# Strassen products summed in PSUM with partial sums copied out between, GpSimd taken out of the token pairs, row block by row block

## The chip, the cores and the metric

One Trainium2 chip, of which the kernel uses one core. The time is the device time of one execution in microseconds (us). Before the change it is 1486.4 us, the median of 3 runs (1483.56 to 1487.43).

## The reference

```python
def reference(**kw):                       # B, H, S, D = 8, 8, 576, 64; d_model 512
    attn_out = _attn_ref(q, k, v)          # block-causal softmax attention
    x = attn_out.transpose(0, 2, 1, 3).reshape(B, S, H * D)
    x = _moe_ref(x, w_val, conv_w, w_out)  # sigmoid(conv(x)) * (x @ w_val) @ w_out
    return _moe2_ref(x, w_ch1, w_ch2)

def _moe2_ref(x, w_ch1, w_ch2):
    X = np.fft.fft(np.fft.fft(x, axis=1), axis=2)
    u = x + np.real(X)
    un = (u - mean(u)) / np.sqrt(var(u) + 1e-06)
    ch = np.maximum(un @ w_ch1, 0.0) @ w_ch2      # 512 -> 2048 -> 512
    return u + ch
```

What matters here is the last line but one: two matrix products with a normalisation before them, for 8 x 576 = 4608 tokens. Every product of numbers of 32 bits is made of three matmuls of a rounded form: high part of the weights with the high and with the low part of the tokens, and the low part of the weights with the high part of the tokens.

## The kernel before, in words

`phase1` does attention, the gated convolution and the Fourier transforms and leaves u in DRAM (`u_d`). `phase2` does the normalisation and the two layers. Its first 1024 tokens are done in two groups of 512 with plain products (loop `for g in range(NG)`). While the second group runs, `combine` forms the sums and differences of weight blocks that Strassen's method wants and stores them in DRAM (`comb_d`, beside the plain blocks in `base_d`).

The other 3584 tokens are done in NQ = 4 *pairs*. A pair is two blocks of N = 448 tokens, and for a pair each layer is one Strassen step (Winograd's form, 2 x 2 blocks): the weights are cut in halves by rows and by columns, the tokens into the two blocks, and seven products stand in place of eight. A pair's work is the list `steps`: (g, l, p, i) is pair g, layer l, product p, row block i, and one step is 12 matmuls of 448 columns (lines 1333 to 1335 in the first layer, 1359 to 1361 in the second). Seven products of four row blocks are 28 steps a layer, 56 a pair, 224 in all: 2688 matmuls. The order of products is `L1O`, `L2O`; within a product the four row blocks i follow each other.

Around the steps:

- `load_chunk` loads the weights of two steps (1 MB) from DRAM into one of six places (`ring_w`); a chunk is asked for five chunks ahead.
- `load_x` loads the next pair's tokens X into one of two sets of places, which take turns, and `norm_x` normalises them, a piece after each step, part of it on GpSimd (POOL). `average` (lines 1107, 1108) puts two matmuls with a matrix of ones on TensorE for each mean.
- `sums` makes a product's operand: Strassen's sums of X blocks in the first layer, of h blocks in the second, all on POOL (lines 1277 to 1287). `operand` splits it into high part (ScalarE cast, line 1303) and low part (VectorE, line 1304), three steps ahead (`LOOK`).
- `product` issues the 12 matmuls and takes the result out of PSUM. In the first layer each product lies in one of three bank pairs in turn, and VectorE adds it to running sums h in SBUF (lines 1344, 1346; Relu on ScalarE, line 1349). In the second layer four steps sum up in a bank pair, and VectorE and POOL add the result to e and to the output rows y (lines 1370 to 1389), which `load_y` has filled with u and `store_y` sends out.

The program's text gives a rough order only: a scheduler in the framework puts the instructions of each engine's queue in order. Within a queue order is strict, and so a waiting instruction holds up all behind it; SyncE (SP) issues all the transfers.

Of the kernel before, what the change touches and what calls it, by code (L numbers as in the profile page):

```python
# [8 lines left out]
F32 = mybir.dt.float32  # L9
# [8 lines left out]
def kernel(  # L18
# [1030 lines left out]
    def phase2():  # L1049
        with ExitStack() as c2:  # L1050
# [60 lines left out]
            def norm(u, n, done, hl=None, first=False, pool=None):  # L1111
                pool = pool or nc.vector
# [116 lines left out]
            L1O, L2O = (1, 6, 2, 7, 5, 3, 4), (1, 3, 5, 2, 6, 7, 4)  # L1229
            steps = [(g, l, p, i) for g in range(NQ) for l in range(2) for p in (L1O, L2O)[l] for i in range(4)]  # L1230
# [3 lines left out]
            ring_w = [4, 5, 6, 7, 8, 9]  # L1234
            ring_o = [10, 11, 12, 13]
# [3 lines left out]
            def load_chunk(c):  # L1239
                if 2 * c >= len(steps):  # L1240
                    return
                g, l, p, i = steps[2 * c]
                z = i // 2
                chunk[c] = at(ring_w[c % 6], [P, 4, 2, 256], F32R, "chunk")
                src = SRC[l, p][z][SLOT[l, p]] if (l, p) in SRC else comb_d[l][z][SLOT[p]]
                nc.sync.dma_start(out=chunk[c].bitcast(F32).rearrange("p j y c -> p (j y c)"), in_=src)

            def load_x(g):
                if g >= NQ:
                    return  # L1250
                for z in range(2):
                    n = (2, 3) if g % 2 == 0 else ("U1", "HH")
                    X[g, z] = at(n[z], [P, 4, N], F32, f"X{z}")
                    load_rows(X[g, z], NG * T + 2 * N * g + N * z, N, 0, 4)

            def norm_x(g):
                if g >= NQ:
                    return
                for z in range(2):
                    def scale(r, u=X[g, z]):  # L1260
                        for t in range(4):
                            (nc.gpsimd if t % 2 else nc.vector).tensor_tensor(  # L1262
                                out=u[:, t, :], in0=u[:, t, :], in1=r, op=ALU.mult)
                            yield
                    yield from norm(X[g, z], N, scale, None, False, nc.gpsimd)
# [3 lines left out]
            def sums(k):  # L1269

                g, l, p, i = steps[k]
                if l == 0:
                    xa, xb = X[g, 0], X[g, 1]
                    b11, b21, b12, b22 = xa[:, 0:2], xa[:, 2:4], xb[:, 0:2], xb[:, 2:4]
                    if p == 6:
                        T2[g] = t2 = s3.tile([P, 2, N], F32, tag="st", name="T2")
                        nc.gpsimd.tensor_tensor(out=b12, in0=b12, in1=b11, op=ALU.subtract)
                        nc.gpsimd.tensor_tensor(out=t2, in0=b22, in1=b12, op=ALU.subtract)
                    elif p == 7:
                        nc.gpsimd.tensor_tensor(out=b11, in0=T2[g], in1=b11, op=ALU.subtract)  # L1280
                    elif p == 4:
                        nc.gpsimd.tensor_tensor(out=b21, in0=T2[g], in1=b21, op=ALU.subtract)
                    return {1: b11, 6: T2.get(g), 2: b21, 7: b11, 5: b12, 3: b22, 4: b21}[p]
                a, b, c, d = (hb[z][i // 2][:, i % 2 * 2:i % 2 * 2 + 2] for z in range(4))
                x, y, z = {5: (b, b, a), 6: (d, d, b), 7: (a, d, a), 4: (c, d, c)}.get(p, (None,) * 3)
                if x is not None:
                    nc.gpsimd.tensor_tensor(out=x, in0=y, in1=z, op=ALU.subtract)  # L1287
                return {1: a, 3: d, 5: b, 2: c, 6: d, 7: a, 4: c}[p]

            src, nitem = {}, [0]  # L1290

            def operand(k):
# [4 lines left out]
                if l == 0 and i:  # L1297
                    opnd[k] = opnd[k - 1]
                    return
                x = src.pop(k) if k in src else sums(k)  # L1300
                o = at(ring_o[nitem[0] % 4], [P, 2, 2, N], F32R, "o")
# [7 lines left out]
            def load_y(g, q):  # L1309
                col = NG * T + 2 * N * g + N * (q in (12, 22))  # L1310
                for m in range(2):
                    if q == 21 and m == 0:
                        Y["pair"] = yp.tile([P, 2, N], F32, tag="y", name="y")
                    Y[q, m] = y = (Y["pair"][:, m] if q == 21 else
                                   kp.tile([P, S], F32, tag={12: "K0", 22: "K1", 11: "KP"}[q], name="y")[:, 0:N])
# [6 lines left out]

            def product(k):
                g, l, p, i = steps[k]
                o, w = opnd.pop(k), chunk[k // 2]
                if l == 0:
                    ps = banks[(k + 2) % 3]
                    for jj in range(2):
                        j = i % 2 * 2 + jj
                        for t in range(2):  # L1330
                            wh, wl = (w[:, j, y, t * P:t * P + P] for y in range(2))
                            to = ps[:, jj, 0:N]
                            nc.tensor.matmul(to, wh, o[:, 0, t], start=(t == 0), stop=False)  # L1333
                            nc.tensor.matmul(to, wh, o[:, 1, t], start=False, stop=False)  # L1334
                            nc.tensor.matmul(to, wl, o[:, 0, t], start=False, stop=(t == 1))  # L1335
                    ps = ps[:, :, 0:N]
                    a, b, c, d = (hb[z][i // 2][:, i % 2 * 2:i % 2 * 2 + 2] for z in range(4))
                    if p == 1:
                        nc.scalar.copy(out=a, in_=ps)  # L1339
                        return  # L1340
                    for to, x in {6: ((b, a),), 2: ((a, a),), 7: ((c, b),), 5: ((d, c), (b, b)), 3: ((b, b),),
                                  4: ((c, c),)}[p]:
                        if p == 4:
                            nc.vector.tensor_tensor(out=to, in0=x, in1=ps, op=ALU.subtract)  # L1344
                        else:
                            nc.vector.tensor_tensor(out=to, in0=ps, in1=x, op=ALU.add)  # L1346
                    if p in (2, 5, 3, 4):
                        h = {2: a, 5: d, 3: b, 4: c}[p]
                        nc.scalar.activation(out=h, in_=h, func=AF.Relu)  # L1349
                    return  # L1350

                ps = banks[(k // 4 + 2) % 3]
                for jj in range(2):
                    j = i % 2 * 2 + jj
                    for m in range(2):
                        wh, wl = (w[:, j, y, m * P:m * P + P] for y in range(2))
                        to = ps[:, m, 0:N]
                        first, final = i == 0 and jj == 0, i == 3 and jj == 1
                        nc.tensor.matmul(to, wh, o[:, 0, jj], start=first, stop=False)  # L1359
                        nc.tensor.matmul(to, wh, o[:, 1, jj], start=False, stop=False)  # L1360
                        nc.tensor.matmul(to, wl, o[:, 0, jj], start=False, stop=final)  # L1361
                if i < 3:
                    return
                add, sub = ALU.add, ALU.subtract
# [224 lines left out]
```

## Time and profile before

| | |
|---|---|
| median of 3 runs | 1486.4 us |
| the profiled execution: its time, its span | 1490.79 us, 1489.0 us |
| granted TensorE clock, mean | 0.977 |
| busy share PE, DVE, ACT, POOL | 93%, 80%, 53%, 36% |
| matmuls of the four pairs | from 883.2 us to 1484.8 us |
| after the last matmul | two VectorE adds, two stores |

A busy time counts every instruction from its start to its modelled end. Matmuls overlap, so that their pitch (start to start, about 0.205 us here) and not their duration (0.37 us) tells how long TensorE needs. An idle time is put down to the instruction that ended it.

### The profile page before, as it was taken

What the parts mean: (1) busy time and instruction counts of PE and PEld (TensorE: products, weight loads), DVE (VectorE), ACT (ScalarE), POOL (GpSimd) and SP (SyncE); (2) the same over time, 40 slices, a digit from 0 to 9 for tenths busy, and PEclk for the clock granted to TensorE, in tenths of its full rate; (3) what the DMA queues carried; (4) which work ended last, traced back from release to release, by engine and by line L of the source; (5) the groups of instructions that cost most, each with busy time, mean ns of one, the idle gap of its engine ahead of it and who ended that gap; (6) DMA issues with size and microseconds to landing.
All of it is one profiled execution on the core that took longest, in us unless ns stands there. A gap on an engine that the chain in (4) does not pass through costs nothing. (4 is left out here: it accounts for less than half of the span.)

```text
span 1489.0 us, 24090 instructions
## 1 busy us (share of the span) xinstructions
PE 1385.4 (93%) x8547; PEld 1215.6 (82%) x8547; DVE 1184.9 (80%) x1873; ACT 786.8 (53%) x1738; POOL 539.1 (36%) x348
## 2 busy tenths in 40 slices
PE   5798999999999999987999987989999999999998
PEld 3576888999898989876876776879988898989987
DVE  5777797979797979898897887988779877975685
ACT  5677777787777777642442333433434343433342
POOL 3323232323232323221001333584438543841283
PEclk9899999999999999998999999999999999999999
DMA  7567665656565656465968957667765675667562
GB/s 210 146 158 211 155 175 148 170 152 170 148 168 151 169 150 178 146 236 192 352 237 284 371 201 293 210 220 272 274 221 197 228 270 195 216 234 262 206 219 85
DMA packets 169603, 308.24 MB, mean 207 GB/s; under 512 B 29310, under 2 KB 108940, under 8 KB 155148
## 3 DMA queue, kind: packets, MB, share of 16 engines
q1 hardware_dynamic: 168944, 306.57, 64.3%
q8 instruction: 68, 1.11, 0.3%
q14 instruction: 51, 0.42, 0.1%
q10 hardware_dynamic: 540, 0.14, 0.0%
HBM read 203.74 MB, written 56.76 MB: 175 GB/s over the span
## 5 line engine op out<-in xcount | busy, mean ns | idle before, releaser
L1304 DVE TENSOR_TENSOR o<-h,o 128x896 fp32r<-128x896 f32 x112 | 208.3, 1888 | 30.8 <-ACT o L1303 30.8
L1287 POOL TENSOR_TENSOR h<-h 128x896 f32<-128x896 f32 x64 | 168.3, 2643 | 95.9 <-ACT h L1349 62.9
L1303 ACT CAST o<-h 128x896 fp32r<-128x896 f32 x112 | 105.4, 943 | 171.0 <-PE banks L1361 131.3
L473 ACT ACTIVATE PB<-sc,mx 128x128 f32<-128x128 f32 (+4 forms) x320 | 166.9, 527 | 51.1 <-DVE mx L459 27.8
L1360 PE MATMUL banks<-o,chunk 128*128 128x448 f32 x448 | 167.2, 373 | 12.2 <-DVE o L1304 12.2
L1333 PE MATMUL banks<-o,chunk 128*128 128x448 f32 x448 | 166.3, 371 | 6.3 <-ACT h L1339 5.5
L1359 PE MATMUL banks<-o,chunk 128*128 128x448 f32 x448 | 166.0, 371 | 2.9 <-DVE h L1344 2.9
L1334 PE MATMUL banks<-o,chunk 128*128 128x448 f32 x448 | 166.1, 371 | 1.5 <-DVE o L1304 1.5
L1361 PE MATMUL banks<-o,chunk 128*128 128x448 f32 x448 | 166.0, 371 | 0.0
L1335 PE MATMUL banks<-o,chunk 128*128 128x448 f32 x448 | 165.9, 370 | 0.0
L587 PE MATMUL pt<-ident,PB 128*128 128x128 f32 x800 | 142.0, 283 | 15.2 <-ACT PTb L593 8.0
L638 POOL TENSOR_TENSOR XL<-XF,XH 128x576 fp32r<-128x576 f32 x32 | 45.9, 1434 | 251.6 <-ACT XH L57 251.3
L1346 DVE TENSOR_TENSOR h<-banks,h 128x896 f32<-128x896 f32 x96 | 102.4, 1082 | 39.8 <-PE banks L1335 39.8
L587 PEld LDWEIGHTS pt<-ident,PB 128*128 128x128 f32 x800 | 101.0, 144 | 32.0 <-ACT PTb L593 14.7
L642 DVE SCALAR_TENSOR_TENSOR gate<-XF,cw,gate 128x575 f32<-128x575 f32 (+3 forms) x128 | 123.2, 963 | 4.3 <-ACT gate L63 3.6
L459 DVE TENSOR_REDUCE mx<-sc 128x1 f32<-128x384 f32 (+2 forms) x192 | 104.1, 560 | 4.2 <-PE sc L193 2.4
L1360 PEld LDWEIGHTS banks<-o,chunk 128*128 128x128 f32 x448 | 85.5, 191 | 23.4 <-DVE o L1304 16.1
L427 PE MATMUL sc<-K,QQ 128*128 128x256 f32 (+2 forms) x256 | 88.0, 354 | 14.5 <-DMA QQ<-QHL 13.4
L1349 ACT ACTIVATE h<-h 128x896 f32<-128x896 f32 x64 | 60.8, 952 | 74.8 <-DVE h L1346 50.7
L1333 PEld LDWEIGHTS banks<-o,chunk 128*128 128x128 f32 x448 | 85.2, 190 | 15.2 <-ACT h L1339 5.9
L593 ACT COPY PTb<-pt 128x512 f32<-128x512 f32 (+1 forms) x160 | 86.8, 546 | 18.9 <-PE pt L587 18.2
L1359 PEld LDWEIGHTS banks<-o,chunk 128*128 128x128 f32 x448 | 85.6, 191 | 10.8 <-DVE h L1344 3.3
(279 smaller groups left out, 3836.4 us busy)
## 6 DMA issues: line engine op xcount, KB each, us to landing
chunk<-comb_d SPq DMA_DIRECT2D x64, 1024.0 KB, 4.9
chunk<-base_d SPq DMA_DIRECT2D x48, 1024.0 KB, 5.0
K<-KP SPq DMA_DIRECT2D x128, 144.0 KB, 2.5
QQ<-QHL SPq DMA_DIRECT2D x128, 128.0 KB, 2.4
comb_d<-packed SPq DMA_DIRECT2D x16, 1024.0 KB, 5.4
rw<-in_w_ch SPq DMA_DIRECT2D x28, 512.0 KB, 6.7
base_d<-W SPq DMA_DIRECT2D x14, 768.0 KB
VV<-in_v SPq DMA_DIRECT2D x32, 320.0 KB, 3.9
```

The costliest lines, as they stand in the source:

```text
L473: nc.scalar.activation(out=PB[i][:, k0:k0 + w], in_=t, func=AF.Exp, bias=nm, accum_out=su[:, at + j:at + j + 1])
L587: nc.tensor.transpose(ps[:, j, :], PB[i][:, (j0 + j) * P:(j0 + j + 1) * P], ident)
L642: nc.vector.scalar_tensor_tensor(out=gate[c][:, s:S], in0=XF[:, 0:S - s], scalar=cw[:, c, 4 - s:5 - s], in1=gate[c][:, s:S], op0=ALU.mult, ...
L1287: nc.gpsimd.tensor_tensor(out=x, in0=y, in1=z, op=ALU.subtract)
L1303: nc.scalar.copy(out=o[:, 0], in_=x)
L1304: nc.vector.tensor_tensor(out=o[:, 1], in0=x, in1=o[:, 0].bitcast(F32), op=ALU.subtract)
L1333: nc.tensor.matmul(to, wh, o[:, 0, t], start=(t == 0), stop=False)
L1334: nc.tensor.matmul(to, wh, o[:, 1, t], start=False, stop=False)
L1335: nc.tensor.matmul(to, wl, o[:, 0, t], start=False, stop=(t == 1))
L1359: nc.tensor.matmul(to, wh, o[:, 0, jj], start=first, stop=False)
L1360: nc.tensor.matmul(to, wh, o[:, 1, jj], start=False, stop=False)
L1361: nc.tensor.matmul(to, wl, o[:, 0, jj], start=False, stop=final)
```

## The change

- **Order of steps.** In the first layer a row block gets all its seven products before the next row block begins. The second layer keeps product after product. Both orders of products are new.
- **Sums in PSUM.** Products of one output go into the same bank without clearing it: 1, then 6 on top, then 7, then 4 (and 5, then 3; product 2 alone). Between them ScalarE (first layer, lines 1378 and 1388 of the new file) or VectorE adds (second layer, line 1396) copy the partial sum out. The signs of some sums change so that only additions are left.
- **No GpSimd in the pairs.** `sums` is gone: `source` and `early` form the same sums on VectorE (line 1278), and `norm_x`, e and y use VectorE alone.
- **Places.** Four places for weights in place of six, eight for operands in place of four (the first layer now holds all seven operands), one set of places for X in place of two. In the first layer a chunk is two transfers of 512 KB.

```diff
-            L1O, L2O = (1, 6, 2, 7, 5, 3, 4), (1, 3, 5, 2, 6, 7, 4)
-            steps = [(g, l, p, i) for g in range(NQ) for l in range(2) for p in (L1O, L2O)[l] for i in range(4)]
+            L1O, L2O = (1, 2, 6, 5, 7, 3, 4), (1, 3, 6, 5, 7, 2, 4)
+            steps = []
+            for g in range(NQ):
+                steps += [(g, 0, p, i) for i in range(4) for p in L1O]
+                steps += [(g, 1, p, i) for p in L2O for i in range(4)]
...
-            ring_w = [4, 5, 6, 7, 8, 9]
-            ring_o = [10, 11, 12, 13]
+            ring_w = [4, 5, 6, 7]
+            ring_o = [10, 11, 12, 13, 8, 9, "U1", "HH"]
...
-                    n = (2, 3) if g % 2 == 0 else ("U1", "HH")
-                    X[g, z] = at(n[z], [P, 4, N], F32, f"X{z}")
+                    X[g, z] = at((2, 3)[z], [P, 4, N], F32, f"X{z}")
...
+            def minus(to, x, y):
+                nc.vector.tensor_tensor(out=to, in0=x, in1=y, op=ALU.subtract)
...
+            def early(g, l, n):
+                if l == 0 and n >= 8 and (n - 8) % 7 == 0:
+                    a, b, c, d = quarters((n - 8) // 7)
+                    minus(b, b, a)
...
+                if 3 <= n < 7:
+                    a, b, c, d = quarters(n - 3)
+                    minus(d, d, b)
+                if 8 <= n < 12:
+                    a, b, c, d = quarters(n - 8)
+                    minus(a, d, a)
+                if 18 <= n < 22:
+                    a, b, c, d = quarters(n - 18)
+                    minus(c, c, d)
...
+            turn = [1, 0, 2]
             def product(k):
...
+                if p == 1 and (l == 0 or i == 0):
+                    turn.insert(0, turn.pop())
+                ps = banks[turn[{1: 0, 6: 0, 7: 0, 4: 0, 5: 1, 3: 1, 2: 2}[p] if l == 0 else
+                                {1: 0, 6: 0, 7: 0, 4: 0, 3: 1, 2: 1, 5: 2}[p]]]
...
+                begin = p in ((1, 5, 2) if l == 0 else (1, 3, 5, 2))
...
+                        first = first and begin
+                        nc.tensor.matmul(to, wh, o[:, 0, x], start=first, stop=False, skip_group_check=not begin)
...
+                    if p in (1, 6, 5, 7):
+                        nc.scalar.copy(out={1: a, 6: b, 5: d, 7: c}[p], in_=ps)
+                    if p == 7:
+                        add(out=d, in0=c, in1=d, op=ALU.add)
+                    if p in (2, 3):
+                        x = a if p == 2 else b
+                        add(out=x, in0=ps, in1=x, op=ALU.add)
+                    if p in (2, 7, 3):
+                        x = {2: a, 7: d, 3: b}[p]
+                        nc.scalar.activation(out=x, in_=x, func=AF.Relu)
+                    if p == 4:
+                        nc.scalar.activation(out=c, in_=ps, func=AF.Relu)
...
+                    for q in {1: (11,), 3: (12,), 6: (12,), 5: (12, 22), 7: (22,), 2: (11,), 4: (21,)}[p]:
+                        add(out=Y[q, m], in0=x, in1=Y[q, m], op=ALU.add)
```

The scheduler moves instructions with this. Three places:

First, ScalarE's queue where the first pair begins (o is an operand's high part, packed the weight sums of `combine`, banks the PSUM results, h the running sums). Before:

```order
L1222 CAST packed<-two 128x4x256
L1339 COPY h<-banks_9325 128x896
L1222 CAST packed<-two 128x4x256
L1303 CAST o<-T_10798 128x896
L1339 COPY h<-banks_9323 128x896
L1303 CAST o<-X_10210 128x896
```

With the change:

```order
L1333 CAST o<-T_10754 128x896
L1378 COPY h<-banks_9325 128x896
L1222 CAST packed<-two 128x4x256
L1333 CAST o<-X_10210 128x896
L1378 COPY h<-banks_9325 128x896
L1386 ACTIVATE h<-h 128x896
L1333 CAST o<-h 128x896
L1378 COPY h<-banks_9324 128x896
```

Bank pair 9325 is copied out, summed into and copied out again; on TensorE six matmuls of product 6 stand right behind product 1, ahead of product 2, and wait for that first copy.

Second, SP's queue around the load of the fourth pair's X (X_12866 and X_12869 before, X_12876 and X_12879 with the change; u_d is their source, y and out the output rows). Before:

```order
L1246 DMA chunk<-comb_d_88 128x2048
L1093 DMA X_12869<-u_d_64 128x4x448
L1246 DMA chunk<-comb_d_87 128x2048
L1246 DMA chunk<-comb_d_88 128x2048
L1093 DMA X_12866<-u_d_63 128x4x320
L1246 DMA chunk<-base_d_85 128x2048
L1093 DMA X_12866<-u_d_64 128x4x128
```

With the change:

```order
L1256 DMA chunk<-comb_d_87 128x1024 x2
L1093 DMA X_12879<-u_d_64 128x4x448
L1349 DMA out<-y 128x448 x2
L1093 DMA X_12876<-u_d_63 128x4x320
L1093 DMA X_12876<-u_d_64 128x4x128
L1256 DMA chunk<-base_d_85 128x1024
L1256 DMA chunk<-base_d_83 128x1024 x2
```

Before, this load stood in the first layer of the second pair. Now it waits for the third pair's operands, which are read from the same places, and stands behind the stores of the second pair's last output rows (they wait for VectorE).

Third, VectorE's queue where that X is first read (line 1114). Before:

```order
L1105 TENSOR_TENSOR al<-q,ah 128x448
L1114 TENSOR_TENSOR s_12886<-X_12866 128x448
L1346 TENSOR_TENSOR h<-banks_9325,h 128x896
L1137 RECIPROCAL r<-r 128x448
L1346 TENSOR_TENSOR h<-banks_9323,h 128x896
```

With the change:

```order
L1396 TENSOR_TENSOR y<-banks_9325,y 128x448 x2
L1383 TENSOR_TENSOR h<-banks_9324,h 128x896
L1114 TENSOR_TENSOR s_12900<-X_12876 128x448
L1115 TENSOR_TENSOR s<-X_12876 128x448
L1334 TENSOR_TENSOR o<-h,o 128x896
L1116 TENSOR_TENSOR s<-s,s_12900 128x448
L1105 TENSOR_TENSOR al<-s,ah 128x448
```

The first reader of X now comes two products into the pair, right behind the last adds to y (line 1396) and the first add to h.

## Rows read from the trace of the kernel before

**Rows 1.** The page's first line
```profile
span 1489.0 us, 24090 instructions
```

**Rows 2.** Timeline of PE: start us, us, line; eight half pairs' first matmuls, the last matmul
```profile
883.21 0.36 PE L1333 MATMUL banks<-o,chunk 128*128 128x448 f32 x1
...
970.19 0.37 PE L1359 MATMUL banks<-o,chunk 128*128 128x448 f32 x1
...
1047.03 0.36 PE L1333 MATMUL banks<-o,chunk 128*128 128x448 f32 x1
...
1123.55 0.66 PE L1359 MATMUL banks<-o,chunk 128*128 128x448 f32 x1 [2.87 <-DVE h L1344]
...
1195.89 0.36 PE L1333 MATMUL banks<-o,chunk 128*128 128x448 f32 x1
...
1270.27 0.36 PE L1359 MATMUL banks<-o,chunk 128*128 128x448 f32 x1
...
1344.02 0.37 PE L1333 MATMUL banks<-o,chunk 128*128 128x448 f32 x1
...
1413.46 0.37 PE L1359 MATMUL banks<-o,chunk 128*128 128x448 f32 x1
...
1484.41 0.36 PE L1361 MATMUL banks<-o,chunk 128*128 128x448 f32 x1
```

**Rows 3.** Waits of PE, 883.2 to 1484.8 us: us in total, times, longest
```profile
PE banks L1360 <- DVE o L1304: 12.2, 10, 5.2
PE pv L1107 <- ACT ah L1104: 6.0, 4, 1.6
PE banks L1333 <- ACT h L1339: 5.5, 1, 5.5
PE banks L1359 <- DVE h L1344: 2.9, 1, 2.9
PE pv L1108 <- DVE al L1105: 2.3, 3, 1.5
```

**Rows 4.** Stretches: length, busy PE, PEld, DVE, ACT, POOL, PEclk, DMA share, GB/s
```profile
883.20:1484.80 601.60, 570.12 (x2713) 514.54 (x2711) 476.48 (x384) 231.47 (x270) 307.68 (x151) 0.98 0.64 225
...
903.90:908.20 4.30, 4.30 (x12) 3.87 (x13) 1.01 (x2) 0.76 (x1) 0.00 (x0) 0.50 1.00 314
```

**Rows 5.** Groups by line, 883.2 to 1484.8 us, VectorE: busy, mean ns of one
```profile
L1304 DVE TENSOR_TENSOR o<-h,o 128x896 fp32r<-128x896 f32 x112 | 208.3, 1888 | 30.8 <-ACT o L1303 30.8
L1346 DVE TENSOR_TENSOR h<-banks,h 128x896 f32<-128x896 f32 x96 | 102.4, 1082 | 39.8 <-PE banks L1335 39.8
...
L1137 DVE RECIPROCAL r<-r 128x448 f32<-128x448 f32 x6 | 17.7, 2946 | 0.5 <-ACT r L1136 0.5
...
L1124 DVE TENSOR_TENSOR X<-X,pm 128x448 f32<-128x448 f32 x24 | 13.8, 611 | 7.5 <-PE pm L1108 7.5
```

**Rows 6.** Timeline of all engines, two low parts on VectorE and GpSimd between them
```profile
1471.23 1.09 DVE L1304 TENSOR_TENSOR o<-h,o 128x896 fp32r<-128x896 f32 x1 [1.10 <-ACT o L1303]
...
1475.86 1.16 POOL L1384 TENSOR_TENSOR y<-y,e 128x448 f32<-128x448 f32 x1 [6.68 <-DVE e L1383]
...
1476.22 1.74 DVE L1304 TENSOR_TENSOR o<-h,o 128x896 fp32r<-128x896 f32 x1
```

**Rows 7.** Groups by line, 883.2 to 1484.8 us, ScalarE and GpSimd
```profile
L1303 ACT CAST o<-h 128x896 fp32r<-128x896 f32 x112 | 105.4, 943 | 171.0 <-PE banks L1361 131.3 <-PE banks L1335 35.6 <-issue 4.1
...
L1339 ACT COPY h<-banks 128x896 f32<-128x896 f32 x16 | 14.4, 908 | 22.2 <-PE banks L1335 21.7 <-DVE packed L1223 0.4
...
L1104 ACT CAST ah<-s 128x448 fp32r<-128x448 f32 x6 | 3.4, 567 | 18.7 <-DVE s L1116 18.7
...
L1464 POOL TENSOR_TENSOR U<-o,U 128x512 f32<-128x512 f32 x4 | 8.0, 2007 | 13.8 <-DVE o L1462 13.8
```

**Rows 8.** DMA issues, 885 to 1489 us: KB each, median us to landing
```profile
chunk<-comb_d SPq DMA_DIRECT2D x62, 1024.0 KB, 4.8
...
X<-u_d SPq DMA_DIRECT2D x2, 896.0 KB, 7.0
```

More of the change, by code (lines that the diff above doesn't have):

```diff
@@ L1241, in load_chunk, with src @@
                     return
[L1242 to L1246, printed above, removed]
+                chunk[c] = at(ring_w[c % len(ring_w)], [P, 2, 2, 2, 256], F32R, "chunk")
+                def src(k):
+                    g, l, p, i = steps[k]
+                    return (SRC[l, p][i // 2][SLOT[l, p]] if (l, p) in SRC else comb_d[l][i // 2][SLOT[p]]), i % 2 * 2 * D
+                to = chunk[c].bitcast(F32).rearrange("p k j y c -> p k (j y c)")
+                if steps[2 * c][1]:
+                    nc.sync.dma_start(out=to.rearrange("p k c -> p (k c)"), in_=src(2 * c)[0])
+                    return
+                for z in range(2):
+                    x, o = src(2 * c + z)
+                    nc.sync.dma_start(out=to[:, z], in_=x[:, o:o + 2 * D])
             def load_x(g):
@@ L1261, in scale @@
                         for t in range(4):
-                            (nc.gpsimd if t % 2 else nc.vector).tensor_tensor(
-                                out=u[:, t, :], in0=u[:, t, :], in1=r, op=ALU.mult)
+                            nc.vector.tensor_tensor(out=u[:, t, :], in0=u[:, t, :], in1=r, op=ALU.mult)
                             yield
-                    yield from norm(X[g, z], N, scale, None, False, nc.gpsimd)
+                    yield from norm(X[g, z], N, scale)
             T2 = {}
-            def sums(k):
-                g, l, p, i = steps[k]
[L1272 to L1288, printed above, removed]
@@ L1352, in product @@
[L1352 to L1361, printed above, removed]
+                o, w = opnd[k], chunk[k // 2]
@@ new lines, in product @@
+                if p == 1 and (l == 0 or i == 0):
+                    turn.insert(0, turn.pop())
+                ps = banks[turn[{1: 0, 6: 0, 7: 0, 4: 0, 5: 1, 3: 1, 2: 2}[p] if l == 0 else
+                                {1: 0, 6: 0, 7: 0, 4: 0, 3: 1, 2: 1, 5: 2}[p]]]
+                z = k % 2 if l == 0 else i % 2
+                begin = p in ((1, 5, 2) if l == 0 else (1, 3, 5, 2))
+                for jj in range(2):
+                    for t in range(2):
+                        wh, wl = (w[:, z, jj, y, t * P:t * P + P] for y in range(2))
+                        if l == 0:
+                            to, x, first, last = ps[:, jj, 0:N], t, t == 0, t == 1
+                        else:
+                            to, x, first, last = ps[:, t, 0:N], jj, i == 0 and jj == 0, i == 3 and jj == 1
+                        first = first and begin
+                        nc.tensor.matmul(to, wh, o[:, 0, x], start=first, stop=False, skip_group_check=not begin)
+                        nc.tensor.matmul(to, wh, o[:, 1, x], start=False, stop=False, skip_group_check=not begin)
+                        nc.tensor.matmul(to, wl, o[:, 0, x], start=False, stop=last, skip_group_check=not begin)
```

111 lines of the change are left out of this document (40 added, 71 removed).

## The prediction

> **What bounds the kernel now.** The change touches the four pairs only, so I went first to the timeline of TensorE and marked where each half pair (one layer of one pair, 28 steps, 336 matmuls) begins [rows 2]. The reader is to see eight differences. They are 86.98, 76.84, 76.52, 72.34, 74.38, 73.75, 69.44 and, up to the end of the last matmul at 1484.77, 71.31 us: 601.6 us of the span of 1489.0 us [rows 1]. The seventh half has neither a norm nor a wait: 69.44 / 336 = 0.2067 us a matmul. That is the floor of a half as long as the number of matmuls stays, and the change keeps all 2688. Eight floors are 555.5 us. The norms of pairs 2 to 4 put 24 more matmuls on TensorE, at 0.2067 us another 5.0 us. So 601.6 - 560.5 = 41.1 us is waiting and what follows from waiting, and nothing else is there to be won: 15.9, 5.4 and 3.3 us in the first layers of pairs 1 to 3 and 7.4, 2.9, 4.3 and 1.9 us in the four second layers.
>
> Next, the waits of TensorE in that stretch say for whom it waited [rows 3]: low parts of operands from VectorE 12.2, a copy by ScalarE 5.5, h from VectorE 2.9, the norms' operands 6.0 + 2.3; these and the small ones that are left out make some 31 us. The other 10 us are slow pitch: after the wait of 5.5 us, twelve matmuls took 4.3 us at a granted clock of 0.50, which is 1.2 GHz [rows 4], about 1.8 us more than at 1.00.
>
> Why is VectorE late, at 476.5 busy us in 601.6 [rows 4]? Its group of low parts has a mean of 1888 ns [rows 5], but a low part that ran with POOL idle took 1.09 us, and one that ran while POOL added to y took 1.74 us [rows 6]. The running sums of the same width, with one input from PSUM, keep a mean of 1082 ns [rows 5]. So an instruction of VectorE with both inputs in SBUF pays up to 0.8 us for POOL's company, and POOL works 307.7 us of this stretch [rows 4].
>
> **The change part by part, VectorE.** POOL does nothing in the pairs any more; its last work is four adds of 2.0 us as the first pair begins [rows 7]. VectorE then has for a pair: 35 low parts, 20 Strassen sums (4 of X, 16 of h), and 12 running sums in place of 28, all of 896 columns: 67 x 1.08 = 72.4 us. 16 adds to y of 448 columns: 16 x 0.61 = 9.8 us, at the price of the X - mean row [rows 5]. Two norms, each of 16 instructions of 448 columns and a reciprocal of 2.95 us [rows 5]: 25.4 us. Sum 107.6 us where TensorE needs 2 x 69.44 = 138.9 us; before it was 476.5 / 4 = 119 us. VectorE takes over POOL's work and still gets lighter.
>
> **Second layers.** The heaviest run is the fourth to twelfth step: 9 low parts, 8 sums, 4 adds, 17 x 1.08 + 4 x 0.61 = 20.8 us in 9 x 2.48 = 22.3 us. Operands may run seven steps ahead (eight places), and I find them some 12 us early at the layer's first steps. The banks that products 6, 7 and 4 return to have been free for four steps. I take 0 for waits here (16.5 us now); the other end is what the fourth pair still shows, 1.9 us in each.
>
> **First layers, the hand-overs.** Within a row block products 6, 7, 4 and 3 are summed onto a bank that ScalarE has to copy first. One product of 2.48 us lies between, the copy takes 0.91 us [rows 7], and I allow 0.1 us for each of the two signals: some 1.4 us to spare, covered by that product between. Nothing on the path, unless ScalarE is late (second rival).
>
> **First pair's beginning.** Before, one operand fed four steps; now seven operands and four sums of X are due within 17 us, while VectorE ends the weight sums and POOL still runs its four adds. Six matmuls of product 6 stand right behind product 1 and wait the whole copy: 1.1 us. Following VectorE's new order at 1.08 us, and three instructions at about 2 us beside POOL, product 7's low part is done 2 us after it is wanted. With 1 us of slow pitch: 4 us, between 0 and the 10 us that I count there now.
>
> **Norms.** X of the next pair has one set of places now, so its load waits for this pair's last operand, about when the pair begins, and stands in SP's queue behind the stores of y: issued some 2 us into the pair, landing 7.0 us later [rows 8], at 9. Three sums on VectorE (1.9 us) and a cast (0.57 us [rows 7]) follow: 11.5. In the second pair TensorE's order has the mean's first matmul after 47 matmuls, 9.7 us: it waits 1.8 us, and 0.6 us more for the low part, 2.5 us. In the third it stands after 56, 11.6 us: 1 us at most. In the first pair the same count, from a start that is late already, gives 3 us. Ends: 0, and for each of the three the landing time once more, 7 us. The second norms of each pair have six steps or more to spare.
>
> **Weights.** Four places leave 6 steps, 14.9 us, between request and use; a chunk lands in 4.8 us [rows 8]. Covered, also with X's 7.0 us ahead of it. The stage before the pairs gains 12 adds on VectorE (7.3 us) and loses POOL's company: 0, within 5 us to either side.
>
> **The sum.** Before: 601.6 us. After: 555.5 + 5.0 + 4 + 3 + 2.5 + 1 = 571.0 us. That is 30.6 us less. The profiled execution took 1490.8 us, 4.4 us above the median of 1486.4; taken from the median the forecast is **1456 us**. All waits gone would be 1445; every term at its far end (10 + 3 x 7, and 4 x 1.9) takes 28 us of it back: 1484.
>
> **Rival 1: the load of X is later still.** At a pair's beginning X (1.8 MB), rows of y both ways and the chunks all move; if two chunks of 4.8 us each go first, X lands 10 us later. VectorE's first reader of X stands ahead of its running sums, the cast ahead of ScalarE's copies, so TensorE stops: three times 10 us and 2 us of half clock, 36 us. For it: the new order of SP. Against it: chunks asked for earlier have mostly landed by then. 1456 + 36 = 1492 us, chance 0.08; half of that is inside the range.
>
> **Rival 2, slower: ScalarE late at the hand-overs.** Four to a row block, 16 row blocks, 64 in all. From 1.4 us of delay on, that is two casts of 0.94 us or one cast that waits for VectorE ahead of the copy, TensorE stops. If a whole copy shows each time: 64 x 0.91 = 58 us, 1456 + 58 = 1514 us. Against it: four copies and four Relu of that width, at 0.94 us at most 7.5 us, in 17.3 us of a row block, and the order puts a waiting cast ahead of a copy only around the norms. The Trainium skill speaks for this rival (Perfetto Trace Analysis, Optimizing Tensor Performance, Matmuls): groups of matmuls that do not depend on each other should go through different PSUM banks in turn, so that taking one out overlaps the next; here products return to the bank just taken out, and by that rule the sum would be this rival's. The order leaves one product of another bank between, which is why I hold the row's 0.91 us for covered: chance 0.05.
>
> **Rival 3: POOL is not what makes VectorE slow.** Then the 59 instructions with both inputs in SBUF stay at 1.89 us: 111.5 + 8.6 + 35.2 = 155 us a pair, above TensorE's 138.9, and VectorE is the bound: 4 x 155 = 620 us, 18 more than now, 1505 us. It decides from a mean of 1.61 us on. The rows with and without POOL speak against it [rows 6]: 0.04.
>
> **How the numbers follow.** Forecast 0.83, almost all of it faster; the rivals 0.08, 0.05 and 0.04. A measurement of this kernel tells 0.3%, 4.5 us, from no change. Of the forecast 0.81 is faster and 0.02 the same; of rival 1, 0.05 faster (late by half), 0.02 same and 0.01 slower; of rival 2, 0.02 same (a part of the hand-overs) and 0.03 slower; of rival 3, 0.01 same and 0.03 slower. In all 0.86, 0.07, 0.07. The range 1443 to 1478 leaves out the terms' farthest ends and the rivals at full price.
>
> **What would show it.** Low parts at 1.08 us throughout; POOL empty after the first pair's beginning; second layers within 1 us of 69.4; waits of TensorE on the norms' cast two products to four into a pair; no wait of the accumulating matmuls on ScalarE's copies. It is wrong if TensorE waits for copies in every row block, or if a half of the fourth pair, which has no norm, takes over 71 us.

## The result and the profile after

The changed kernel takes 1449.5 us, the median of 4 runs (1446.95 to 1450.48), against 1485.0 us before: a ratio of 0.976, 95% interval 0.9735 to 0.9781. The forecast was 1456 us, the range 1443 to 1478. Two of the ten executions of f6 below (2687 and 6026 us) and one of the kernel before (1545.4 us) were far slower than all others of the same kernel, and no median or ratio here counts them. The profiled execution took 1450.48 us. The first lines of its page, then TensorE's timeline at the eight halves and the last matmul (start us, us), to lay beside [rows 2]:

```profile
span 1448.7 us, 24001 instructions
## 1 busy us (share of the span) xinstructions
PE 1374.4 (95%) x8547; PEld 1211.8 (84%) x8547; DVE 1097.9 (76%) x1945; ACT 822.2 (57%) x1778; POOL 220.0 (15%) x188
```

```profile
876.66 0.36 PE L1370 MATMUL banks<-o,chunk 128*128 128x448 f32 x1
...
948.99 0.36 PE L1370 MATMUL banks<-o,chunk 128*128 128x448 f32 x1
...
1017.08 0.37 PE L1370 MATMUL banks<-o,chunk 128*128 128x448 f32 x1
...
1094.13 0.37 PE L1370 MATMUL banks<-o,chunk 128*128 128x448 f32 x1
...
1163.57 0.37 PE L1370 MATMUL banks<-o,chunk 128*128 128x448 f32 x1
...
1236.03 0.37 PE L1370 MATMUL banks<-o,chunk 128*128 128x448 f32 x1
...
1305.47 0.37 PE L1370 MATMUL banks<-o,chunk 128*128 128x448 f32 x1
...
1374.91 0.37 PE L1370 MATMUL banks<-o,chunk 128*128 128x448 f32 x1
...
1444.14 0.37 PE L1372 MATMUL banks<-o,chunk 128*128 128x448 f32 x1
```

The halves take 72.3, 68.1, 77.1, 69.4, 72.5, 69.4, 69.4 and 69.6 us, together 567.8 us where it was 601.6: 33.8 us less. The other 6.5 us of the 40.3 by which the span is shorter lie before the pairs, which begin at 876.66 instead of 883.21. Now TensorE's waits in the pairs, to lay beside [rows 3], and the same stretch by engines, beside [rows 4]:

```profile
PE pm L1107 <- ACT ah L1104: 7.0, 2, 5.3
PE banks L1370 <- ACT h L1378: 1.0, 1, 1.0
PE banks L1370 <- DMA chunk<-comb_d: 0.6, 1, 0.6
```

```profile
876.60:1444.50 567.90, 559.35 (x2713) 509.47 (x2712) 388.08 (x436) 264.50 (x307) 7.83 (x4) 1.00 0.70 239
```

Of the 12.2 us for low parts, 5.5 us for a copy and 2.9 us for h nothing is left; the norms' operand, 6.0 us before (and 2.3 for its low part), is 7.0. Why VectorE is no longer late is read from its groups, beside [rows 5], with ScalarE's copies of partial sums (mean ns of one behind the comma):

```profile
L1334 DVE TENSOR_TENSOR o<-h,o 128x896 fp32r<-128x896 f32 x112 | 120.8, 1085 | 44.7 <-ACT o L1333 44.3
L1278 DVE TENSOR_TENSOR h<-h 128x896 f32<-128x896 f32 x64 | 68.8, 1087 | 9.6 <-ACT h L1386 9.2
L1383 DVE TENSOR_TENSOR h<-banks,h 128x896 f32<-128x896 f32 x32 | 34.8, 1087 | 32.5 <-PE banks L1372 32.5
```

```profile
L1378 ACT COPY h<-banks 128x896 f32<-128x896 f32 x64 | 58.0, 906 | 59.9 <-PE banks L1372 59.7
```

The low part fell from 1888 to 1085 ns, the sum with one input in PSUM stayed at 1.08 to 1.09 us. VectorE is busy for 388 us of the pairs instead of 476, with the sums, norms and adds to y that POOL had. The Trainium skill (SBUF — State Buffer, Who interferes with whom) says that a VectorE instruction with two inputs in SBUF contends with GpSimd's reads and one with at most one input there, outside the two-port performance modes, does not; these two groups agree.

That fits the forecast. But it does not yet tell which part of the change earned it.

### The profile page after: what moved, and what is told of

It reads as the page before. It is cut to its first block, busy times and chain, and to the rows that moved or that the text cites. A ratio compares the mean times of both kernels' runs of the same rounds, so it can differ in the third digit from the quotient of the medians.

```text
span 1448.7 us, 24001 instructions
## 1 busy us (share of the span) xinstructions
PE 1374.4 (95%) x8547; PEld 1211.8 (84%) x8547; DVE 1097.9 (76%) x1945; ACT 822.2 (57%) x1778; POOL 220.0 (15%) x188
## 4 chain that ended last, share of the span: by engine, by line
PE 70%; DVE 12%; DMA 7%; ACT 4%; issue 3%; POOL 2%; SPq 2%; POOLq 0%; DVEq 0%; ACTq 0%
PE banks L1372 12%; PE banks L1370 12%; PE banks L1371 11%; PE av L615 4%; PE pt L587 4%; PE sc L427 2%; DVE gate L642 2%; PE banks L1441 2%; PE banks L1442 2%; PE sc L428 2%; PE banks L1443 2%; PE banks L1461 1%; PE banks L1459 1%; PE banks L1460 1%; PE psx L191 1%
## 5 line engine op out<-in xcount | busy, mean ns | idle before, releaser
L1370 PEld LDWEIGHTS banks<-o,chunk 128*128 128x128 f32 x896 | 168.5, 188 | 17.9 <-ACT h L1378 1.4
L1372 PEld LDWEIGHTS banks<-o,chunk 128*128 128x128 f32 x896 | 168.5, 188 | 15.8
L1371 PEld LDWEIGHTS banks<-o,chunk 128*128 128x128 f32 x896 | 168.5, 188 | 15.7
L1334 DVE TENSOR_TENSOR o<-h,o 128x896 fp32r<-128x896 f32 x112 | 120.8, 1085 | 44.7 <-ACT o L1333 44.3
L1378 ACT COPY h<-banks 128x896 f32<-128x896 f32 x64 | 58.0, 906 | 59.9 <-PE banks L1372 59.7
L191 PE MATMUL psx<-GH,we_h 128*128 128x290 f32 x256 | 83.6, 327 | 2.4 <-ACT GH L57 1.5
L191 PE MATMUL psv<-XH,wv_h 128*128 128x288 f32 x256 | 83.5, 327 | 0.4 <-ACT PB L473 0.4
L428 PE MATMUL sc<-KL,QQ 128*128 128x256 f32 (+2 forms) x256 | 83.5, 336 | 0.0
L192 PE MATMUL psx<-GL,we_h 128*128 128x290 f32 x256 | 76.2, 298 | 0.5 <-DVE GL L703 0.5
L192 PE MATMUL psv<-XL,wv_h 128*128 128x288 f32 x256 | 76.2, 298 | 0.0
```

The source lines that it names most:

```text
L191: nc.tensor.matmul(ps, lh, rh, start=first, stop=False)
L192: nc.tensor.matmul(ps, lh, rl, start=False, stop=False)
L428: nc.tensor.matmul(t[:, o:o + w], q[:, 1, m], KL[p][:, 0:w], start=False, stop=True)
L1334: nc.vector.tensor_tensor(out=o[:, 1], in0=x, in1=o[:, 0].bitcast(F32), op=ALU.subtract)
L1370: nc.tensor.matmul(to, wh, o[:, 0, x], start=first, stop=False, skip_group_check=not begin)
L1371: nc.tensor.matmul(to, wh, o[:, 1, x], start=False, stop=False, skip_group_check=not begin)
```

## The experiments

The theory at the start: POOL beside VectorE made operands late, and both the removal of POOL and the sums in PSUM (fewer running sums) help. The rivals: the order and the sums do the work, or one part alone does, or a part costs. The table gathers what follows; "places" are those for the second layer's operands, "others" the pairs' norms and adds to y. Ratios are to the kernel before on the same chip, with 95% intervals; "pairs" is the time from the first to the last matmul of the four pairs in the profiled execution.

| kernel | sums | others | order | places | median us | ratio | pairs us |
|---|---|---|---|---|---|---|---|
| before | POOL | POOL | old | 4 | 1485.0 | | 601.6 |
| f6 | POOL | VectorE | old | 4 | 1479.6 | 0.996 (0.9942 to 0.9986) | 600.6 |
| g2 | POOL | VectorE | new | 4 | 1485.3 | 0.998 (0.9959 to 0.9999) | 603.4 |
| e1 | POOL | VectorE | new | 8 | 1454.8 | 0.979 (0.9772 to 0.9811) | 574.5 |
| f5 | VectorE | POOL | old | 4 | 1449.7 | 0.977 (0.975 to 0.9797) | 563.8 |
| the change | VectorE | VectorE | new | 8 | 1449.5 | 0.976 (0.9735 to 0.9781) | 567.8 |
| f1, the change again | VectorE | VectorE | new | 8 | 1447.6 | 0.9745 (0.9727 to 0.9763) | 567.7 |
| e2 | VectorE | VectorE | old | 4 | 1439.5 | 0.9685 (0.9666 to 0.9704) | 558.4 |
| f2, e2 again | VectorE | VectorE | old | 4 | 1439.6 | 0.969 (0.9671 to 0.9702) | 558.4 |

**POOL taken out, and nothing else (e2, f2).** The kernel before, every `nc.gpsimd` of the pairs made `nc.vector`:

```diff
-                    nc.gpsimd.tensor_tensor(out=x, in0=y, in1=z, op=ALU.subtract)
+                    nc.vector.tensor_tensor(out=x, in0=y, in1=z, op=ALU.subtract)
```

and likewise in lines 1262 to 1282, 1371, 1384 and 1387.

> The kernel before with every GpSimd instruction of the pairs moved to VectorE, no sums in PSUM. Theory: VectorE then has 35 low parts, 20 sums and 28 running sums of 1.08 us, 22 adds of 0.61 us and norms of 25.4 us a pair, 128 us where TensorE needs 138.9; low parts at 1.08 us, most waits gone, 1450 to 1462 us, second layers within 2 us of 69.4. Rival (sums in PSUM are what brought the gain, VectorE cannot take GpSimd's work without them): 1475 us or more.

> The kernel before with all of POOL's work in the pairs given to VectorE, once more. Theory that taking POOL out gives the whole gain, and that the rest of the change (sums in PSUM, row blocks, one set of X places) costs: 1438 to 1442, 7 to 12 us below the change on the same chip; of these some 5 to 8 are waits of the norms and the rest pitch. Rival that the 10 us were the pitch of the executions alone: within 4 us of the change this time.

1439.5 and 1439.6 us, less than e2's theory gave and in f2's range. This small edit beats the whole change by 8 to 10 us. Its waits of TensorE in the pairs, all in the first pair, and the pairs by engines are:

```profile
PE banks L1333 <- ACT h L1339: 1.9, 1, 1.9
PE banks L1334 <- DVE o L1304: 1.1, 1, 1.1
PE banks L1333 <- DVE o L1462: 0.8, 1, 0.8
PE banks L1359 <- DVE h L1344: 0.5, 1, 0.5
PE banks L1360 <- DVE o L1304: 0.5, 1, 0.5
```

```profile
876.20:1434.60 558.40, 553.47 (x2713) 508.58 (x2711) 465.43 (x531) 231.76 (x270) 6.85 (x4) 1.00 0.69 242
```

So VectorE carries all 28 running sums of a pair and POOL's work too, busy for 465 of 558 us, and is hardly ever late. The sums in PSUM were not needed for that.

**Which of POOL's work (f5, f6).** f5 moves Strassen's sums alone (lines 1277 to 1287), f6 moves all but these.

> The kernel before with only Strassen's sums moved from POOL to VectorE (80 instructions of 1.08 us there in place of 211 us on POOL); norms and adds to y stay on POOL, some 100 us. Theory A: what held TensorE was that the sums on POOL took longer (2.64 us) than a step (2.48 us) and slowed VectorE beside them: most of the 46 us comes with this part alone, 1443 to 1458; the stage before the pairs keeps its POOL work and stays 5 us longer. Rival B: the adds to y and the norms on POOL are the harm: 1468 or more.

> The other part: the kernel before with norms and adds to y moved to VectorE and Strassen's sums left on POOL. With sums on POOL the changed kernel took 1454.8 us. Theory A (the old order asks for a sum each step, three steps ahead, four operand places; a sum of 2.64 us on POOL and a slowed low part then come late): the waits in the second layers stay, 1466 to 1482. Rival B (the order doesn't matter, norms and adds to y were the harm): 1450 to 1460, second layers at 69.5 us or less.

Both times lie where theory A put them. The sums alone bring 34 us, the rest alone some 4 us. In f6 TensorE waits for low parts again. The line of waits, then VectorE's and POOL's groups, then a part of the timeline:

```profile
PE banks L1360 <- DVE o L1304: 17.4, 13, 5.1
```

```profile
L1304 DVE TENSOR_TENSOR o<-h,o 128x896 fp32r<-128x896 f32 x112 | 182.5, 1655 | 31.2 <-ACT o L1303 31.2
...
L1287 POOL TENSOR_TENSOR h<-h 128x896 f32<-128x896 f32 x64 | 163.2, 2561 | 263.3 <-ACT h L1349 223.6 <-DVE o L1304 38.3
```

```profile
1128.35 3.03 DVE L1304 TENSOR_TENSOR o<-h,o 128x896 fp32r<-128x896 f32 x1
1131.30 4.96 DVE L1371 TENSOR_TENSOR y<-y,e 128x448 f32<-128x448 f32 x2
...
1139.19 0.74 PE L1360 MATMUL banks<-o,chunk 128*128 128x448 f32 x1 [5.05 <-DVE o L1304]
```

The mean of 1.66 us hides two kinds of low part: 59 of the 112 ran with POOL idle and took 1.09 us, and beside a sum of POOL one took up to 3.03 us, longer than a step (2.43 to 2.48 us). Adds to y of 448 columns took 2.5 us there, where [rows 5] has 0.61 for that width. The low parts that ended the 13 waits all ran without a gap behind VectorE's other work, and 11 of them took 2.9 to 3.0 us: VectorE was late because it was slow, not because it stood waiting for a sum. Nor does a sum on POOL take longer than a step by itself: in e1 below those that ran with VectorE idle took 2.1 us. And the old order doesn't ask for the sums three steps ahead, as f6's expectation has it, but 8 to 12 (lines 1477 to 1482); only casts and low parts are three ahead. f5 against e2, 10 us, is what the norms and adds to y still cost on POOL: by the profiles 4.3 us lie before the pairs, where only the first pair's norm is on POOL, and 5.4 in the pairs.

**The change with its sums on POOL (e1).**

```diff
             def minus(to, x, y):
-                nc.vector.tensor_tensor(out=to, in0=x, in1=y, op=ALU.subtract)
+                nc.gpsimd.tensor_tensor(out=to, in0=x, in1=y, op=ALU.subtract)
```

> The changed kernel with the 80 Strassen sums (20 a pair) on GpSimd again, everything else as in the change. Theory (GpSimd's company makes VectorE's instructions with two SBUF inputs slow, and that made TensorE wait): low parts go from a mean of 1085 ns to between 1400 and 1900 ns, waits of TensorE on low parts come back in the second layers, 1460 to 1480 us. Rival (the sums in PSUM alone brought the gain, GpSimd is harmless): within 5 us of the changed kernel's 1449.5 us.

1454.8 us: it costs 5 to 7 us, less than the theory gave it and a little more than the rival, and all of it in the first half, which takes 81.3 us; the second layers take 69.1, 69.1, 69.1 and 68.3. The slowness is there, in the second layer of the first pair six low parts in a row at 2.8 us each (the timeline's line below); the lateness is not:

```profile
L1334 DVE TENSOR_TENSOR o<-h,o 128x896 fp32r<-128x896 f32 x112 | 187.3, 1709 | 43.4 <-ACT o L1333 43.0
...
L1278 POOL TENSOR_TENSOR h<-h 128x896 f32<-128x896 f32 x64 | 168.0, 2644 | 287.5 <-ACT h L1386 222.4 <-DVE o L1334 64.5
```

```profile
960.44 16.68 DVE L1334 TENSOR_TENSOR o<-h,o 128x896 fp32r<-128x896 f32 x6
```

```profile
PE pm L1107 <- ACT ah L1104: 5.9, 2, 4.0
PE banks L1370 <- DVE o L1471: 3.7, 1, 3.7
PE banks L1370 <- ACT h L1378: 3.6, 1, 3.6
PE banks L1370 <- issue: 1.1, 3, 0.4
```

No wait for a low part of the second layer, at 1709 ns in the mean. So the rest of the change cures the same illness by another way. Which part of it?

**Four places instead of eight (g2).** e1, and the second layer's operands in four places:

```diff
-                o = at(ring_o[nitem[0] % len(ring_o)], [P, 2, 2, N], F32R, "o")
+                m = nitem[0] % 35
+                o = at(ring_o[(m + 4) % 8 if m < 7 else m % 4], [P, 2, 2, N], F32R, "o")
```

> The change with its sums on POOL, as before in this study (1454.8 us), but the operands of the second layer take turns in four places, as in the kernel before, in place of eight. Theory: with sums on POOL it is the lead that eight places give which keeps TensorE fed though a sum takes 2.64 us and a low part 1.7 us; with four, the second layers rise from 69.1 to 72 to 78 us each, the time to 1465 to 1490. Rival: it is VectorE's lighter load (12 running sums a pair in place of 28) and the sums asked for earlier; then second layers stay at 70 us or less, time 1453 to 1459.

1485.3 us: the theory holds, and the whole gain is gone. The second layers of pairs 1 to 3 take 77.9, 77.9 and 78.7 us, and the wait is back:

```profile
PE banks L1372 <- DVE o L1335: 15.7, 11, 2.4
PE banks L1371 <- DVE o L1472: 4.7, 1, 4.7
```

Ten of these eleven waits lie in second layers. Three low parts had been slow themselves (3.0 us); before the other seven VectorE waited for a cast by ScalarE, and that one for a sum on POOL (in the second pair's, 4.9 and 4.2 us). So here the sums are late as well, not VectorE alone.

New order, sums in PSUM, lighter VectorE, and the one set of places for X that goes with them: with POOL's sums and four places they are worth, taken together, nothing that can be measured well (0.2%; the pairs take 603.4 us, in f6 600.6). The change thus holds two cures for one illness, POOL out (46 us alone) and eight places (in the new order, with norms and y off POOL, 30 us), and each makes the other nearly superfluous. Eight places in the old order were not tried.

**The hand-overs (e4, f4).** e4 puts product 6 right behind product 1; f4 lets ScalarE copy each partial sum twice.

```diff
-            L1O, L2O = (1, 2, 6, 5, 7, 3, 4), (1, 3, 6, 5, 7, 2, 4)
+            L1O, L2O = (1, 6, 2, 5, 7, 3, 4), (1, 3, 6, 5, 7, 2, 4)
```

```diff
-                        nc.scalar.copy(out={1: a, 6: b, 5: d, 7: c}[p], in_=ps)
+                        for _ in range(2):
+                            nc.scalar.copy(out={1: a, 6: b, 5: d, 7: c}[p], in_=ps)
```

> The changed kernel with product 6 right after product 1 in every row block of the first layers, so that its matmuls wait for the copy of product 1 with nothing between. Theory (a hand-over costs the copy of 0.91 us and two signals, and the product between hides it all): 15 row blocks more at 1.1 us, 16 to 18 us, 1466 to 1468 us. Rival (TensorE's queue or the other half bank hides part of it anyway): 1449 to 1458 us.

> The change, but ScalarE copies each partial sum out of PSUM twice in a row: 64 more copies of 0.91 us, 58 us more of ScalarE. Theory of the prediction (a hand-over has 2.48 us of another product to cover 0.91 us and two signals, some 1.4 us to spare): 1.82 us still fit; TensorE waits for copies in the first pair's beginning only, time within 4 us of the change. Rival (products that return to the bank just copied have no slack; ScalarE is near late): each of the 64 hand-overs shows up to 0.9 us, time 20 to 58 us above the change.

e4: 1448.8 us, no change; the theory missed, and the rival's time came for another reason than the rival's. The scheduler did not leave the place empty: in 14 of the 16 row blocks it put 4 to 6 matmuls of product 2 between, 0.8 to 1.2 us, and that is cover enough for a copy of 0.91 us. In two row blocks of the first pair product 6 does stand right behind product 1, and there each hand-over cost a copy's length (waits of TensorE in e4's pairs):

```profile
PE banks L1370 <- ACT h L1378: 2.0, 2, 1.0
```

So rival 2 had the price of a bare hand-over right; there are hardly any bare ones. f4: 1449.5 us, within 0.3% of the change, as the theory said. The copies are there twice, one timeline row of two and their group:

```profile
1312.53 1.85 ACT L1379 COPY h<-banks 128x896 f32<-128x896 f32 x2 [0.95 <-PE banks L1372]
...
L1379 ACT COPY h<-banks 128x896 f32<-128x896 f32 x128 | 115.7, 909 | 41.8 <-PE banks L1372 40.7
```

and TensorE waited for one of them once, 0.5 us. A covered hand-over has over 0.9 us to spare: the copy could take that much longer.

**The norms (e3, g1, f1).** The change is 8 to 10 us behind e2 though its VectorE is lighter. e3 begins the norms seven steps later; g1 leaves out the normalisation of pairs 2 to 4, so that these compute on u itself.

```diff
                     load_x(g + 1)
+                    nxt = iter(())
+                if n == 7:
                     nxt = norm_x(g + 1)
```

```diff
             def norm_x(g):
-                if g >= NQ:
+                if g >= NQ or g > 0:
```

> The changed kernel with the next pair's norm begun seven steps into the pair instead of at its start (its load is asked for as before). Theory (the two waits of 5.3 and 1.7 us on the norm's cast come from X landing late): both go, with about 1 us of slow pitch, 1441 to 1443 us. Rival (the wait moves to the norm's next part or to the second layer, where the norm now ends): 1447 to 1451 us.

> The change without the normalisation of pairs 2 to 4 (they compute on u as it is; 24 matmuls, 96 adds and multiplications, 6 reciprocals less). Theory: what the changed kernel loses against the kernel with POOL alone taken out is the norms' doing, by their two waits (5.3 and 1.7 us with what follows) and by the longer pitch, which begins at a norm's matmul: the halves of pairs 2 to 4 come to 68.1 us each but for a matmul's wait, the pairs take 552 to 555 us instead of 567.8, the time is 1432 to 1437. Rival (the longer pitch has another cause, such as the places of operands or chunks): second layers of pairs 2 to 4 and the fourth pair stay at 69.44, pairs 558 to 561 us, time 1439 to 1443.

> The change once more, unaltered, with a profile of its own. In the first profile the matmuls of gap-free stretches followed each other either every 0.2027 us or every 0.2067 us, at a granted clock of 1.00 in both; 1500 of the 2688 stood at the longer pitch. Theory: the pitch is of the execution, not of the kernel; then the stretches at 0.2067 us lie elsewhere this time, and the executions spread by some 3 to 5 us (1444 to 1451). Rival: it belongs to the kernel's order; then pairs 2 to 4 have second layers of 69.44 us again, all executions within 1.5 us of 1449.5.

First, the wait. In the second pair of the change X is asked for behind the stores, 3.1 us into the pair, and its first reader runs 12.5 us into it:

```profile
1017.99 2.09 SPq L1349 DMA_DIRECT2D out<-y  x2
1020.14 1.77 SPq L1093 DMA_DIRECT2D X<-u_d  x2
...
1029.57 0.63 DVE L1114 TENSOR_TENSOR s<-X 128x448 f32<-128x448 f32 x1 [6.26 <-DMA X<-u_d]
...
1032.04 0.74 PE L1107 MATMUL pm<-ah,ones 128*128 128x448 f32 x1 [5.27 <-ACT ah L1104]
```

Then seven matmuls at a granted clock of 0.50, the 1.2 GHz level. e3 took 1445.9 us, against the change's 1449.5 and 1447.6: between what its theory and its rival gave. TensorE doesn't wait for the norm's operand there, but ScalarE does: the norm's cast waits 4.7 us for X and holds up a copy behind it, and TensorE waits 2.7 us for that copy (ScalarE's timeline in e3):

```profile
1026.45 0.90 ACT L1378 COPY h<-banks 128x896 f32<-128x896 f32 x1
1032.08 0.56 ACT L1104 CAST ah<-s 128x448 fp32r<-128x448 f32 x1 [4.72 <-DVE s L1116]
1032.55 1.71 ACT L1378 COPY h<-banks 128x896 f32<-128x896 f32 x2
```

In e3's profiled execution (1448.6 us) waits and half clock cost 4.8 us less than in the change's, but the longer of the two pitches that come next costs 3.2 us more.

Second, the pitch. The half from 948.99 to 1017.08 and the one from 1094.13 to 1163.57 have 336 matmuls each, no wait, and this (stretches by engine):

```profile
949.00:1017.00 68.00, 68.00 (x337) 63.04 (x336) 55.69 (x61) 27.55 (x30) 0.00 (x0) 1.00 0.70 236
1094.20:1163.50 69.30, 69.30 (x337) 62.94 (x336) 55.51 (x60) 27.45 (x30) 0.00 (x0) 1.00 0.70 234
```

The same work at the same granted clock of 1.00 (2.4 GHz), and 1.35 us apart: 0.2027 us a matmul in the one, 0.2067 in the other. f1's theory, that this is of the execution, fell: its halves are those of the first profile within 0.4 us (the executions spread by 4.4 us all the same, more than its rival allowed), and in both the longer pitch sets in at the same matmul, that of a norm, at 1066 and at 1064 us. In g1, without those norms, every half from the second on takes 68.1 us, 1427.5 us in all: its theory of the cause holds, and the gain is larger than its range. The first rows here are of the change, the norm's two matmuls where the longer pitch begins; the last one is g1's pairs:

```profile
1066.05 0.36 PE L1107 MATMUL pm<-ah,ones 128*128 128x448 f32 x1
1066.25 0.36 PE L1108 MATMUL pm<-al,ones 128*128 128x448 f32 x1
1066.45 0.37 PE L1370 MATMUL banks<-o,chunk 128*128 128x448 f32 x1
```

```profile
876.10:1423.10 547.00, 545.54 (x2689) 504.51 (x2687) 318.04 (x334) 242.71 (x265) 7.83 (x4) 1.00 0.72 248
```

So the norms of three pairs, measured by leaving them out, cost the changed kernel 567.8 - 547.0 = 20.8 us: 4.9 for 24 matmuls, 6.7 for the longer pitch (over all halves, mean pitch less 0.2027, times 336), and the remaining 9.2 us for waits and half clock. In e2, by the same sums from its timeline, the pitch costs 2.0 us, and waits and half clock cost 4.8 us less than in the change: that is the 9.4 us between the two kernels' pairs. In e2 no matmul of a norm waits: with two sets of places the third pair's tokens are asked for from 943 to 953 us, some 70 us before the second pair begins, in the change with one set from 1017 to 1021 us. No run gave the change its second set back, so that the set's price is read from these timelines and not tried.

**The stage before the pairs (f3).** The change, with the first pair's norm on POOL as before:

```diff
-                            nc.vector.tensor_tensor(out=u[:, t, :], in0=u[:, t, :], in1=r, op=ALU.mult)
+                            (nc.gpsimd if g == 0 and t % 2 else nc.vector).tensor_tensor(
+                                out=u[:, t, :], in0=u[:, t, :], in1=r, op=ALU.mult)
...
-                    yield from norm(X[g, z], N, scale)
+                    yield from norm(X[g, z], N, scale, None, False, None if g else nc.gpsimd)
```

> The change, but the first pair's norm has its additions and half of its multiplications on POOL as before. Theory: these beside VectorE are what delayed the stage before the pairs; the first pair then begins at 881 to 884 instead of 876.7, and the time is 4 to 7 us above the change. Rival: the 6.5 us came from the change of order in the stage before the pairs (fewer chunks loaded ahead, the order of VectorE): the pairs begin at 876 to 878, time as the change within 2 us.

1458.7 us, 11 us above the change on the same chip, more than either said, and the pairs begin at 877.1, which would be the rival's. The clock time misleads: this execution was 4.7 us ahead when the stage began. From the stage's first matmul to the pairs' it is 883.21 - 679.65 = 203.6 us before, 876.66 - 679.55 = 197.1 with the change and 877.14 - 674.88 = 202.3 in f3. TensorE's waits on VectorE in the stage, of before, of the change and of f3:

```profile
PE banks L1432 <- DVE HL L1437: 9.0, 5, 3.8
```

```profile
PE banks L1441 <- DVE HL L1446: 3.8, 1, 3.8
```

```profile
PE banks L1442 <- DVE HL L1447: 7.2, 6, 3.5
```

So 5.2 of the 6.5 us are gone again with that norm on POOL. One of them lies in the stage's first group, where the edit does nothing; the second group alone takes 103.3 us before, 96.8 with the change, 101.0 in f3 and 101.1 in f5, whose norms are on POOL too, so that some 4 us are the norm's. The larger part of f3's loss is in the pairs, 577.7 us: the norms' waits lie elsewhere (2.7, 2.2 and 5.3 us), and the pitch is the longer one in all second layers. Why they moved was not found.

## Why the prediction was right, step by step

- **What bounds the kernel:** right in kind, off in the floor. 69.44 us was a half at the longer pitch; the floor is 68.1 us, 8 x 68.1 = 544.8. The step read one half without waits as the least a half can take. That the terms nearly met is luck: 555.5 was given, 544.8 + 6.7 of pitch = 551.5 was found.
- **VectorE:** right. Low parts at 1085 ns were said to be 1.08 us; rival 3 falls with that, and f6 and e1 show means of 1.66 and 1.71 us when POOL's sums return. The price of POOL's company was too low: "up to 0.8 us" was read beside an add to y of half the width, and beside the sums it is up to 1.9 us (3.02 us before the change, 3.03 in f6, against 1.09). The sum used such a price in the first pair's beginning alone.
- **Second layers, 0 us:** right, no wait in any of the four. One of them, at the shorter pitch, is 1.3 us off the 69.4 that was given within 1 us.
- **Hand-overs, 0 us:** right, and f4 shows that there is room. The rule from the Trainium skill (Perfetto Trace Analysis, Optimizing Tensor Performance, Matmuls) that stood behind rival 2 gives no price; rival 2, priced from rows, would have cost 58 us. The trace has one wait of 1.0 us, at the bare hand-over where the prediction had put its 1.1, and e4 has two of 1.0. For bare hand-overs the rule and the trace agree; one other product between, or a third to a half of one, is rotation enough.
- **First pair's beginning and norm, 4 + 3 us:** too high. That half is 72.3 us, 2.6 above 68.1 and the norm's matmuls (1.6).
- **Norms of pairs 2 and 3, 2.5 + 1 us:** too low, the mis-sized term. By the same account they cost 6.8 and 2.0 us. Two of the load's four pieces were issued 3.1 us into the pair where 2 was said, and the larger of them landed 9.3 us later where 7.0 was said; TensorE wanted the mean at 9.7 and got it at 15.0. In place of rival 1's 10 us it was late by some 3.5 us beyond the estimate in the second pair and 0.7 in the third; e3 shows the chain that rival described.
- **The stage before the pairs, 0 within 5 us:** missed by a little. The 12 adds on VectorE cost less than POOL's company did: 6.5 us gained, of which f3 takes 4 to 5 back.
- **The sum:** 571.0 us for the pairs was said, 567.8 found. Errors of both signs met: the floor with its pitch was 4.0 us too high, the first pair 4.4 too high, the norms 5.3 too low. With the stage's 6.5 us the profiled executions differ by 40.3 us where 30.6 was said; the medians differ by 35.5, because the profiled execution of before lay 5.8 us above the median of 1485.0 and that of the change 1.0 above its own.

What the prediction did not ask is whether the parts add up. It laid the 30 us on the change as a whole; e2 and g2 show that one part of it, POOL out of the pairs, gives 46 us, and that the rest of the change adds nothing to that and gives 8 to 10 us back. That these go to the one set of places for X, and to where the norms fall in TensorE's order, is read from timelines and from g1, and not tried by itself.

## What to carry to other kernels

When an engine that feeds TensorE is late, ask first what its instructions take with and without a neighbour at work (one by one: a mean mixes the two), and price that part of a change alone: here the plain move off GpSimd beats the rewrite that contained it (1439.5 us against 1449.5 and 1447.6). A slow feeder can be cured by speed or by lead (more places), and doing both pays once. And places taken for one buffer come from another: X's second set was given up for the operands' lead, and the second and third pair have a wait for X near their beginning that the kernel with two sets (e2) doesn't have.

## What the runs showed of the hardware that was not expected

- A stream of 448-column matmuls without waits runs at one of two pitches, 0.2027 or 0.2067 us, at the same granted clock of 1.00 (and at 0.95, which the profile of e3 shows through its pairs). In the change and in e2 it keeps the one until a wait or the matmuls of a norm, and may go on at the other behind them, at the same places in two executions of the same kernel. Why one place changes it and another doesn't was not found: of eight pairs of a norm's matmuls in the change that stand directly behind each other, two began the longer pitch, and in e4 it changes in the fourth pair as well, which has no norm. It may not be fixed for every kernel either: f4's profiled execution took 1442.5 us with the shorter pitch in its second layers, its five others 1449.0 to 1450.9, and those have no profile.
- A low part of 1.09 us takes up to 3.0 us beside POOL's sums, in the new order as in the old, and the means of 1.66 to 1.71 us in f6, g2 and e1 mix it with those that ran alone. The sums pay too: 2.1 us with VectorE idle, up to 3.0 beside it (e1). A running sum with one input in PSUM took at most 1.09 us in all of them. TensorE hardly shows it with eight places for operands; with four it shows at once.
- Which of f5's 5.4 us over e2 in the pairs the adds to y cost and which the norms was not tried apart.
